# One table orders every operation of local attention and gated convolution, in smaller pieces

## The chip, the core and the metric

The kernel runs on one core of a Trainium2 chip. The metric is the device time of one execution in microseconds, less is better. TensorE (PE) multiplies, VectorE (DVE), ScalarE (ACT) and GpSimd (POOL) work on elements, SyncE (SP) issues the DMAs. Each engine takes its own queue in order and waits at an instruction until what it needs is there.

## The reference

For 4 batches, 8 heads, 768 positions and 64 dimensions: each query attends to the keys less than 16 positions away and to 24 block summaries (the maximum of the keys of 32 positions, the mean of the values). The result `x` goes through a causal depthwise convolution of 5 taps, whose sigmoid gates a projection of `x`; a second projection gives the output.

```python
k_sum = k.reshape(B, H, nb, block, D).max(axis=3)
v_sum = v.reshape(B, H, nb, block, D).mean(axis=3)
scores_l = where(abs(pos_q - pos_k) < 16, scale * q @ k.T, -1e9)
scores_s = scale * q @ k_sum.T + log(block)
a = softmax(concatenate([scores_l, scores_s], -1))
x = a @ concatenate([v, v_sum], 2)               # (B, S, 512)
gate = sigmoid(sum(conv_w[k] * xp[:, k:k + S] for k in range(5)))
out = (gate * (x @ w_val)) @ w_out
```

## The kernel before

The work is cut into 24 units: 4 batches, 3 thirds of the sequence (256 positions), 2 halves of the heads. Two units make a group `g`, 12 in all. Each stage of a unit has a function, called here by a short name that the new table uses too:

- S (`mm_s`, L311): scores on PE, 32 small matmuls, into the one PSUM buffer `s`. Half r holds one pair of heads.
- N (`snorm`, L328): mask and running minimum on DVE, 8 instructions, each with a read of its accumulator.
- E (`exps`, L342): 8 exps with row sums on ACT.
- R and M (`norm`): reciprocal of the sums on DVE (L350, L351), then two multiplications on POOL (L354) into `p`, which has three buffers.
- T and C (`tp` L367, `pcopy` L371): four transposes on PE per half into the one buffer `pt`, and its copy to `pts` on ACT. The second half waits for the first copy.
- X (`mm_x`, L387): probabilities by values on PE into the one buffer `x`.
- H, F and L (`xout`): on ACT the rounded part `xh` (L402) and the full `xf` (L403), on POOL the rest `xl` (L405). h is the halo of `xf` (L286, L288).
- I, A and G (`ginit` L419, `taps` L428, `gate` L436): the convolution. ACT starts the accumulator `g` (one PSUM buffer) with the last tap, DVE adds the other four for each of two head pairs in place, ACT takes the tanh.
- V, gf, gh and gl (`val_mm` L453, `val_ev` L460 and L467, `val_low` L476): value projection on PE (24 matmuls of two split parts; group 0 uses the weights unsplit), gating on DVE, split on ACT and POOL.
- O, oe and st (`out_mm` L491, `out_ev` L505 and L506): output projection on PE, scaling on ACT, store on SP.

`prep_k` makes the block maxima (ks, L129, on DVE) and copies them between the keys (kc, L139, POOL); `prep_v` sums the values on POOL (tr, L153) or DVE; `fill_vs` (f, L200) writes the means into the value tile `v` by DMA; `conv_w` and `split_w` turn the weights' 64-bit words into floats and split them (s, d, e, c, b on ACT, DVE, DVE, ACT, POOL).

The order of every queue is the order in which the program calls these functions: the scheduler is set to manual. The first 8 units are written out by hand, call by call. From unit 8 on `step(s)` is called: it puts X of unit s-2, one or two projections, S, N and E of unit s, T and C of unit s-1, then the taps and the tanh of unit s-2. The loads are a string `LOADS` and tables by step. All DMAs stand in SP's one queue.

Of the kernel before, what the change touches and what calls it, by code (L numbers as in the profile page):

```python
# [57 lines left out]


@with_exitstack  # L60
def tile_attention_then_gated_conv(
# [35 lines left out]
    ktile = {}  # L97
    vtile = {}
    vTt = {}

    def load_q0(pr):
# [11 lines left out]
    def load_vT(b, pr):
        t = ld.tile([P, S], F32, tag="vT", name=f"vT_{b}_{pr}")
        nc.sync.dma_start(t, vT[b, pr])
        vTt[b, pr] = t

    def load_v(g):
# [1 line left out]
        t = ld.tile([VROWS, TPU, DM], F32, tag="v", name=f"v_{g}")  # L120
        for e in range(VP):
            nc.sync.dma_start(t[:, 2 * e : 2 * e + 2], vw[b, th, e])
        vtile[g] = t

    def prep_k(b, pr):
        t = ktile[b, pr]
        ks = wk.tile([P, NB], F32, tag="ks", name=f"ks_{b}_{pr}")
# [47 lines left out]

    def place_vs0():
        for e in range(2):
            ps = ps_p.tile([P, DM], F32, tag="pp", name=f"vb_{e}")
# [4 lines left out]
            vblk[e] = t

    def prep_vs(b):
        ps = ps_p.tile([P, DM], F32, tag="pp", name=f"vsp_{b}")
# [4 lines left out]
        vsum[b] = t

    def fill_vs(g):
        b = g // NTH
        vr = vtile[g].rearrange("p (t e) c -> p e t c", e=2)
        for e in range(2):
            for half in range(2):
                off = OFF_A if (e == half) else OFF_B
                src = vsum[b][half * HB : half * HB + HB] if b else vblk[e][off : off + HB]
                nc.sync.dma_start(  # L200
                    vr[off : off + HB, e],
                    src.unsqueeze(1).broadcast_to([HB, TPU // 2, DM]),
                )
# [657 lines left out]
```

## Time and profile before

| | |
|---|---|
| median of 3 runs | 265.61 us (263.45 to 267.11) |
| span of the profiled execution | 262.0 us |
| around the span (median less span) | 3.6 us |
| busy: PE, ACT, DVE, POOL | 231.1, 193.0, 185.1, 151.8 us |
| instructions | 7326 |
| moved by DMA | 46.39 MB |

The span runs from the first to the last instruction of one profiled execution on the chip. Busy time is the time in which an engine had at least one instruction under way; the rest it waited or had nothing to do. The page lists the chain of work that ended last, and the trace gives each instruction's start, its length and what ended the idle time ahead of it.

### The profile page before, as it was taken

The numbers are of one execution on the slowest core, as the hardware profiler recorded it, in microseconds if no ns is written. First come the engines' busy times: TensorE is split into PE (matmuls) and PEld (weight loads), VectorE is DVE, ScalarE is ACT, GpSimd is POOL, SyncE is SP. The second block draws the span as 40 slices with busy tenths as digits, with TensorE's granted clock in tenths as the row PEclk, the third lists the DMA queues.
The fourth block names the chain that finished last, engine by engine and source line by source line (L and its number), as shares of the span: only waits on it lengthen the run. The fifth ranks groups of instructions, "written<-read, shape, count | busy, mean of one in ns | idle before, by whom it ended". The sixth has DMA issues, their size and how long they took to land.

```text
span 262.0 us, 7326 instructions
## 1 busy us (share of the span) xinstructions
PE 231.1 (88%) x2652; PEld 193.6 (74%) x2652; DVE 185.1 (71%) x692; ACT 193.0 (74%) x619; POOL 151.8 (58%) x212
## 2 busy tenths in 40 slices
PE   1258977889596999999999999999999999997994
PEld 1146866756482689888988898889889988986883
DVE  1866999597966687779776967797778667843610
ACT  1448994966648889888987898889878988875211
POOL 2243087767465788878663888887544744461410
PEclk9999999999777799999999999999999999999999
DMA  6999998175501967726118998171184511111012
GB/s 192 402 404 410 354 354 305 17 290 188 170 8 26 319 238 241 267 51 247 44 22 257 363 329 290 22 280 44 17 261 108 192 58 27 40 43 40 14 70 80
DMA packets 17028, 46.39 MB, mean 177 GB/s; under 512 B 2368, under 2 KB 3392, under 8 KB 16992
## 3 DMA queue, kind: packets, MB, share of 16 engines
q1 hardware_dynamic: 16992, 45.93, 50.9%
q8 instruction: 21, 0.34, 0.5%
q14 instruction: 15, 0.12, 0.2%
HBM read 37.46 MB, written 6.29 MB: 167 GB/s over the span
## 4 chain that ended last, share of the span: by engine, by line
PE 75%; ACT 10%; POOL 5%; issue 4%; DVE 2%; DMA 2%; SPq 0%; POOLq 0%; ACTq 0%; DVEq 0%
PE out L491 27%; PE val L453 22%; PE s L311 9%; PE x L387 8%; PE pt L367 8%; ACT p L342 4%; DMA k<-in_kT_dram 2%; POOL xl L405 2%; POOL p L354 1%; ACT pts L371 1%; DVE sn L328 1%; ACT wv L241 1%; ACT xf L403 1%; DVE ks L129 1%; POOL k L139 1%
## 5 line engine op out<-in xcount | busy, mean ns | idle before, releaser
L428 DVE SCALAR_TENSOR_TENSOR g<-xf,cwt,g 128x256 f32<-128x256 f32 x192 | 93.9, 489 | 13.9 <-ACT g L419 8.0
L342 ACT ACTIVATE p<-sn,nm 128x120 f32<-128x120 f32 x192 | 73.2, 386 | 10.9 <-DVE nm L328 10.9
L354 POOL TENSOR_TENSOR p<-p,ri 128x480 f32<-128x480 f32 x48 | 47.0, 1001 | 42.1 <-DVE ri L351 41.7
L328 DVE CUSTOM_DVE_ANT_0 sn<-s,mask 128x120 f32<-128x120 f32 x192 | 40.9, 278 | 33.3 <-PE s L311 33.3
L453 PE MATMUL val<-xh,wv 128*128 128x256 f32 x352 | 51.8, 289 | 0.7 <-ACT xh L402 0.7
L491 PE MATMUL out<-wo,gh 128*128 128x512 f32 x176 | 49.2, 418 | 2.0 <-ACT wo L241 1.2
L453 PEld LDWEIGHTS val<-xh,wv 128*128 128x128 f32 x352 | 45.6, 192 | 1.6 <-ACT xh L402 1.1
L405 POOL TENSOR_TENSOR xl<-xf,xh 128x512 fp32r<-128x512 f32 x22 | 28.3, 1288 | 23.3 <-ACT xf L403 23.3
L367 PE MATMUL pt<-ident,p 128*120 128x128 f32 x192 | 31.5, 289 | 11.0 <-ACT pts L371 7.6
L491 PEld LDWEIGHTS out<-wo,gh 128*128 128x128 f32 x176 | 32.1, 193 | 11.0 <-POOL wo L242 3.4
L311 PE MATMUL s<-k,qbd 64*64 64x120 f32 x768 | 27.7, 282 | 10.9 <-POOL k L139 10.9
L342 ACT ACTIVATION_READ_ACCUMULATOR p<-sn,nm 128x1 f32 x192 | 36.7, 191 | 0.0
L371 ACT COPY pts<-pt 120x512 f32<-120x512 f32 x48 | 27.6, 575 | 10.3 <-PE pt L367 10.3
L367 PEld LDWEIGHTS pt<-ident,p 128*120 128x120 f32 x192 | 21.7, 142 | 16.6 <-issue 7.3
L387 PEld LDWEIGHTS x<-pts,v 120*64 120x64 f32 x768 | 27.0, 141 | 9.2 <-issue 8.1
L476 POOL TENSOR_TENSOR gl<-gf,gh 128x512 fp32r<-128x512 f32 x22 | 28.5, 1298 | 6.6 <-ACT gh L467 6.6
L311 PEld LDWEIGHTS s<-k,qbd 64*64 64x64 f32 x768 | 20.9, 139 | 14.4 <-POOL k L139 12.6
L453 PE MATMUL val<-xl,wv 128*128 128x256 f32 x176 | 29.6, 288 | 1.8 <-POOL xl L405 1.7
L387 PE MATMUL x<-pts,v 120*64 120x64 f32 x768 | 30.7, 229 | 0.6 <-ACT g L419 0.5
L436 ACT ACTIVATE gt<-g 128x512 f32<-128x512 f32 x24 | 14.4, 599 | 22.0 <-DVE g L428 22.0
L153 POOL TENSOR_TENSOR vT<-vT 128x384 f32<-128x384 f32 (+3 forms) x44 | 25.6, 581 | 2.6
L453 PEld LDWEIGHTS val<-xl,wv 128*128 128x128 f32 x176 | 24.8, 191 | 2.6 <-POOL xl L405 2.1
(53 smaller groups left out, 268.2 us busy)
## 6 DMA issues: line engine op xcount, KB each, us to landing
v<-in_vw_dram SPq DMA_DIRECT2D x24, 512.0 KB
k<-in_kT_dram SPq DMA_DIRECT2D x16, 478.0 KB
vT<-in_vT_dram SPq DMA_DIRECT2D x16, 384.0 KB
out_dram<-ob SPq DMA_DIRECT2D x23, 256.0 KB
qbd<-in_qT_dram SPq DMA_DIRECT2D x11, 512.0 KB
raw_wv<-in_wv_dram SPq DMA_DIRECT2D x4, 512.0 KB
raw_wo<-in_wo_dram SPq DMA_DIRECT2D x4, 512.0 KB
v<-vs SPq DMA_DIRECT2D x36, 48.0 KB
```

What stands on the lines that cost most here:

```text
L311: nc.tensor.matmul(st[u]["sp"][64 * e : 64 * e + 64, h, c * KW : c * KW + KW], qbd[g % NQB][64 * h : 64 * h + 64, pr, i * QT : i * QT + QT ...
L328: nc.vector.tensor_tensor_reduce(s["sn"][:, n, :], s["sp"][:, h, c * KW : c * KW + KW], mask[:, mv, :], -1.0 / math.sqrt(D), 3.0e38, ALU.a ...
L342: nc.scalar.activation(s["p"][:, n, :], s["sn"][:, n, :], AF.Exp, bias=s["nm"][:, n : n + 1], scale=-1.0, accum_out=s["rs"][:, n : n + 1],)
L354: nc.gpsimd.tensor_tensor(s["p"][:, w], s["p"][:, w], ri[:, w].unsqueeze(2).broadcast_to([P, TPU, KW]), ALU.mult,)
L367: nc.tensor.transpose(s["pt"][:KW, i, :], s["p"][:, TPU * r + i, :], ident)
L371: nc.scalar.copy(s["pts"][:, TPU * r : TPU * r + TPU], s["pt"][:KW])
L387: nc.tensor.matmul(dst, v[:KW, i, c0 : c0 + D], src, start=True, stop=g > 0)
L405: nc.gpsimd.tensor_tensor(G["xl"][:, prs, :], x[:, prs, HALO:], G["xh"][:, prs, :].bitcast(F32), ALU.subtract)
L428: nc.vector.scalar_tensor_tensor(gt[:, r], x[:, pr, o : o + SG], cwt[:, pr, o : o + 1], gt[:, r], ALU.mult, ALU.add,)
L453: nc.tensor.matmul(pp[:, r], w, x, start=(n == 0), stop=(n == len(terms) - 1))
L476: nc.gpsimd.tensor_tensor(G["gl"][:, cos, :], gf, G["gh"][:, cos, :].bitcast(F32), ALU.subtract)
L491: nc.tensor.matmul(pp, x, w, start=(n == 0), stop=(n == len(terms) - 1))
```

## The change

All calls are replaced by one table of some 1,400 tokens, `ORDER`, and one small function per operation. A token such as `E.5.2` is unit 5, piece 2; the loop at the end calls the functions in the table's order, so every queue takes its subsequence. Tiles are made where they are first used. The pieces are smaller: N and E come in four pieces of two per unit, A in eight single taps, I in two halves, M in two, a load of `v` in two, a fill in four, and H, F, L, oe, st, gf, gh, gl, ks and kc stand each for itself. The arithmetic, the tile sizes and the buffer counts are the same.

```diff
-LOADS = "k0 q0 m k1 q1 n0 i k2 q2 n1 k3 q3 n2 n3 v0 c Q w0 w1 w2 w3 v1"
+ORDER = """
+k.0.0 q0.0 k.0.3 k.0.1 m q0.1 k.0.2 q0.3 ks.0.0 q0.2 w.3 kc.0.0 S.0.0 c ks.0.3 ks.0.1 q.1 i N.0.0
+n.0.3 kc.0.1 E.0.0 N.0.1 kc.0.3 S.0.1 E.0.1 ks.0.2 n.0.2 n.0.0 N.0.2 n.0.1 kc.0.2 E.0.2 N.0.3
...
-    def step(s, late=lambda: None):
-        u, t, x = s < NU, s - 1 < NU, s - 2 < NU
...
-            mm_s(s, 0)
-            mm_s(s, 1)
-            snorm(s, 0)
-            snorm(s, 1)
-        if t:
-            tp(s - 1, 0)
-        if u:
-            exps(s, 0)
...
+    def op_N(u, c):
+        b, th, hp = units[u]
+        sn = wt(("sn", u), [P, NP, KW], "sn")
+        nm = wt(("nm", u), [P, NP], "nm", bufs=4)
...
+        for h in range(2):
+            n = 2 * c + h
+            nc.vector.tensor_tensor_reduce(
...
+    def op_E(u, c):
+        p = wt(("p", u), [P, NP, KW], "p", bufs=3)
+        rs = wt(("rs", u), [P, NP], "rs", bufs=4)
+        for n in (2 * c, 2 * c + 1):
+            nc.scalar.activation(
...
+    def op_I(u, r):
+        gt = once(("g", u), lambda: ps_g.tile([P, 2, SG], F32, tag="g", name=f"g_{u}"))
...
+    def op_A(u, k):
+        r, o = divmod(k, NK - 1)
+        gt, pr = tiles["g", u][:, r], 2 * (u % NHP) + r
+        nc.vector.scalar_tensor_tensor(
+            gt, xf(u // NHP)[:, pr, o : o + SG], cwt[:, pr, o : o + 1], gt, ALU.mult, ALU.add
+        )
...
+    for token in ORDER.split():
+        name, *at = token.split(".")
+        ops[name](*(int(a) for a in at))
```

Three places of the queues. The names are tile, unit (or group and part) and a running number; `x8` is eight in a row.

ACT at the start, before (`p` is written by exps, `pts` by copies of transposes, `sc` by weight conversion):

```order
L342 ACTIVATE p_0_136,rs_0_138<-sn_0_135,nm_0_137 128x120 x8
L342 ACTIVATE p_1_185,rs_1_187<-sn_1_184,nm_1_186 128x120 x4
L371 COPY pts_0_217<-pt_0_0_218 120x512
L342 ACTIVATE p_1_185,rs_1_187<-sn_1_184,nm_1_186 128x120 x4
L371 COPY pts_0_217<-pt_0_1_240 120x512
L182 ACTIVATE vb0_259<-vb_0_254 120x512
L182 ACTIVATE vb1_266<-vb_1_261 120x512
L213 ACTIVATE sc_cw_285<-cwraw_116 128x20
L213 ACTIVATE sc_wv0_289<-raw_wv0_119 128x512
L371 COPY pts_1_293<-pt_1_0_294 120x512
L213 ACTIVATE sc_wv1_300<-raw_wv1_121 128x512
L403 COPY xf_0_338<-x_0_304 128x2x256
```

and now:

```order
L430 ACTIVATE p_0_133,rs_0_134<-sn_0_125,nm_0_126 128x120 x8
L347 ACTIVATE sc_wv3_184<-raw_wv3_104 128x512
L430 ACTIVATE p_1_204,rs_1_205<-sn_1_197,nm_1_198 128x120 x6
L347 ACTIVATE sc_cw0_236<-cwraw_117 128x20
L372 CAST wv_86<-wf_88 128x512
L430 ACTIVATE p_1_204,rs_1_205<-sn_1_197,nm_1_198 128x120 x2
L430 ACTIVATE p_2_262,rs_2_263<-sn_2_247,nm_2_248 128x120 x6
L454 COPY pts_0_302<-pt_0_0_255 120x512
L430 ACTIVATE p_2_262,rs_2_263<-sn_2_247,nm_2_248 128x120 x2
L347 ACTIVATE sc_wv2_324<-raw_wv2_178 128x512
L347 ACTIVATE sc_wv0_331<-raw_wv0_201 128x512
L454 COPY pts_0_302<-pt_0_1_315 120x512
```

The exps of units 2 and 3 stand ahead of the copies of unit 1 and of the first output of X; weights are taken in the order 3, 2, 0.

PE in the loop, before (one pass from X of unit 9; `s` scores, `pt` transposes, `val` and `out` projections):

```order
L387 MATMUL x_9_1583<-pts_9_1499,v_4_1065 64x64 x16
L311 MATMUL s_11_1621<-k_1_2_645,qbd1_82 64x120 x8
L311 MATMUL s_11_1621<-k_1_3_770,qbd1_82 64x120 x8
L367 MATMUL pt_10_0_1651<-ident_84,p_10_1472 120x128 x4
L453 MATMUL val_4_0_1678<-xh_4_1303,wv_88 128x256 x8
L453 MATMUL val_4_0_1678<-xl_4_1304,wv_88 128x256 x4
L453 MATMUL val_4_0_1678<-xh_4_1303,wv_88 128x256 x8
L453 MATMUL val_4_0_1678<-xl_4_1304,wv_88 128x256 x4
L367 MATMUL pt_10_1_1703<-ident_84,p_10_1472 120x128 x4
L491 MATMUL out_3_0_1723<-wo_89,gh_3_1409 128x512 x8
```

and now, the pass in which T of unit 8 stands:

```order
L450 MATMUL pt_8_0_1336<-ident_84,p_8_1055 120x128 x4
L399 MATMUL s_11_1343<-k_1_2_597,qbd1_82 64x120 x8
L399 MATMUL s_11_1343<-k_1_3_350,qbd1_82 64x120 x8
L467 MATMUL x_7_1366<-pts_7_1282,v_3_866 64x64 x16
L450 MATMUL pt_8_1_1392<-ident_84,p_8_1055 120x128 x4
L550 MATMUL out_1_0_1400<-wo_87,gh_1_1232 128x512 x8
L550 MATMUL out_1_0_1400<-wo_87,gl_1_1279 128x512 x4
L450 MATMUL pt_9_0_1452<-ident_84,p_9_1157 120x128 x4
L399 MATMUL s_12_1459<-k_2_0_1234,qbd0_81 64x120 x8
L399 MATMUL s_12_1459<-k_2_1_921,qbd0_81 64x120 x8
```

S of unit 11 stood beside T of unit 10 and stands beside T of unit 8; there is one projection between the two T pairs here where there were two.

DVE in the loop, before (`sn` masks, `g` taps, `ri` reciprocals, `gf` gating, `ks` maxima):

```order
L328 ISA sn_9_1319,nm_9_1321<-s_9_1318,mask_83 128x120
L328 ISA nm_9_1321 128x1
L328 ISA sn_9_1319,nm_9_1321<-s_9_1318,mask_83 128x120
L328 ISA nm_9_1321 128x1
L428 SCALAR_TENSOR_TENSOR g_7_1308<-xf_3_959,cwt_85,g_7_1308 128x256 x8
L350 TENSOR_SCALAR ri_9_1370<-rs_9_1322 128x8
L351 RECIPROCAL ri_9_1370<-ri_9_1370 128x8
L460 SCALAR_TENSOR_TENSOR gf_3_0_1407<-gt_3_958,val_3_0_1375 128x512
L129 TENSOR_REDUCE ks_2_0_1412<-k_2_0_1016 128x24
L328 ISA sn_10_1471,nm_10_1473<-s_10_1470,mask_83 128x120
L328 ISA nm_10_1473 128x1
L328 ISA sn_10_1471,nm_10_1473<-s_10_1470,mask_83 128x120
```

and now:

```order
L501 SCALAR_TENSOR_TENSOR g_6_1322<-xf_3_1226,cwt_85,g_6_1322 128x256 x6
L415 ISA sn_11_1414,nm_11_1415<-s_11_1343,mask_83 128x120
L415 ISA nm_11_1415 128x1
L415 ISA sn_11_1414,nm_11_1415<-s_11_1343,mask_83 128x120
L415 ISA nm_11_1415 128x1
L501 SCALAR_TENSOR_TENSOR g_6_1322<-xf_3_1226,cwt_85,g_6_1322 128x256
L415 ISA sn_11_1414,nm_11_1415<-s_11_1343,mask_83 128x120
L415 ISA nm_11_1415 128x1
L415 ISA sn_11_1414,nm_11_1415<-s_11_1343,mask_83 128x120
L415 ISA nm_11_1415 128x1
L501 SCALAR_TENSOR_TENSOR g_6_1322<-xf_3_1226,cwt_85,g_6_1322 128x256
L415 ISA sn_11_1414,nm_11_1415<-s_11_1343,mask_83 128x120
```

The eight taps of a unit are broken up by masks of a unit five later; before, eight masks stood in a row ahead of eight taps in a row.

## Rows read from the trace of the kernel before

**Rows 1.** The page: the span, and the busy time of the engines (share of the span, instructions).

```profile
span 262.0 us, 7326 instructions
...
PE 231.1 (88%) x2652; PEld 193.6 (74%) x2652; DVE 185.1 (71%) x692; ACT 193.0 (74%) x619; POOL 151.8 (58%) x212
```

**Rows 2.** Stretches of 20 us: length, busy us of PE, of PE's weight loads, of DVE, ACT and POOL (with the instructions), then the granted clock, the DMA share and GB/s.

```profile
0.00:20.00 20.00, 6.85 (x75) 4.87 (x75) 10.80 (x46) 7.78 (x31) 5.84 (x21) 1.00 0.92 334
20.00:40.00 20.00, 16.55 (x249) 13.94 (x247) 16.69 (x62) 18.12 (x59) 9.40 (x12) 1.00 1.01 374
...
60.00:80.00 20.00, 15.82 (x171) 11.79 (x164) 15.14 (x43) 11.69 (x34) 10.88 (x17) 0.83 0.30 104
...
100.00:120.00 20.00, 20.00 (x238) 17.88 (x237) 16.90 (x74) 17.53 (x61) 17.27 (x26) 1.00 0.59 196
```

**Rows 3.** The chain of waits, one pass of the loop: start, us, engine and line.

```profile
97.67 1.08 PE x L387 x32
98.75 0.98 PE s L311 x32
99.73 0.58 PE pt L367 x4
100.31 2.91 PE val L453 x24
103.22 0.44 PE pt L367 x4
103.66 2.80 PE out L491 x12
```

**Rows 4.** PE in order of time, the first 60 us: start, us, engine, line, operation, out<-in, shapes, count, and in brackets the idle time ahead and what ended it.

```profile
5.50 1.08 PE L311 MATMUL s<-k,qbd 64*64 64x120 f32 x16 [5.50 <-POOL k L139]
...
17.49 1.08 PE L311 MATMUL s<-k,qbd 64*64 64x120 f32 x16 [0.21 <-POOL k L139]
...
30.09 7.17 PE L453 MATMUL val<-xf,wf 128*128 128x256 f32 x32
...
59.56 0.64 PE L311 MATMUL s<-k,qbd 64*64 64x120 f32 x16
```

**Rows 5.** The same, 56 to 100 us and the end.

```profile
69.07 1.08 PE L367 MATMUL pt<-ident,p 128*120 128x128 f32 x4 [3.17 <-ACT pts L371]
...
81.54 0.60 PE L491 MATMUL out<-wo,gh 128*128 128x512 f32 x1 [1.22 <-ACT wo L241]
...
87.19 1.74 PE L491 MATMUL out<-wo,gl 128*128 128x512 f32 x4
...
240.65 0.74 PE L453 MATMUL val<-xh,wv 128*128 128x256 f32 x4 [0.69 <-ACT xh L402]
...
242.49 0.50 PE L453 MATMUL val<-xl,wv 128*128 128x256 f32 x2 [0.87 <-POOL xl L405]
...
257.34 1.10 PE L491 MATMUL out<-wo,gl 128*128 128x512 f32 x4
```

**Rows 6.** One stretch of 2 us, columns as in rows 2.

```profile
84.00:86.00 2.00, 1.96 (x5) 1.00 (x4) 1.67 (x4) 1.97 (x10) 2.00 (x3) 0.50 0.52 94
```

**Rows 7.** The start: the second K tile on the chain of waits (start, us), then the first mask on DVE and the first exp on ACT in order of time.

```profile
2.11 5.50 DMA k<-in_kT_dram
...
6.64 0.28 DVE L328 CUSTOM_DVE_ANT_0 sn<-s,mask 128x120 f32<-128x120 f32 x1 [1.70 <-PE s L311]
...
6.97 0.40 ACT L342 ACTIVATE p<-sn,nm 128x120 f32<-128x120 f32 x1 [4.95 <-DVE nm L328]
```

**Rows 8.** ACT in order of time: two exps in a row, four weight casts, copies of x, a wait for the transposes, and the tanh in the loop with the idle time ahead of it.

```profile
30.79 0.39 ACT L342 ACTIVATE p<-sn,nm 128x120 f32<-128x120 f32 x1
...
31.17 0.39 ACT L342 ACTIVATE p<-sn,nm 128x120 f32<-128x120 f32 x1
...
34.58 2.17 ACT L241 CAST wv<-wf 128x512 fp32r<-128x512 f32 x4
...
42.17 0.59 ACT L402 CAST xh<-x 128x512 fp32r<-128x512 f32 x1 [1.49 <-PE x L387]
42.65 0.59 ACT L403 COPY xf<-x 128x512 f32<-128x512 f32 x1
...
78.58 0.59 ACT L371 COPY pts<-pt 120x512 f32<-120x512 f32 x1 [2.64 <-PE pt L367]
...
96.88 0.60 ACT L436 ACTIVATE gt<-g 128x512 f32<-128x512 f32 x1 [0.92 <-DVE g L428]
```

**Rows 9.** DVE in order of time, one pass of the loop: the last mask of a unit, eight taps, and what stands behind them.

```profile
101.22 0.28 DVE L328 CUSTOM_DVE_ANT_0 sn<-s,mask 128x120 f32<-128x120 f32 x1
...
101.42 4.16 DVE L428 SCALAR_TENSOR_TENSOR g<-xf,cwt,g 128x256 f32<-128x256 f32 x8
105.49 0.16 DVE L350 TENSOR_SCALAR ri<-rs 128x8 f32<-128x8 f32 x1
...
106.38 0.95 DVE L129 TENSOR_REDUCE ks<-k 128x24 f32<-128x768 f32 x1
```

**Rows 10.** SP's waits (us in total, times, longest), and its issues in order of time.

```profile
SPq L200 <- DMA v<-in_vw_dram: 13.8, 5, 5.9
...
147.02 3.31 SPq L200 DMA_DIRECT2D v<-vs  x4
...
152.74 0.88 SPq L122 DMA_DIRECT2D v<-in_vw_dram  x2
```

More of the change, by code (lines that the diff above doesn't have):

```diff
@@ L95, in tile_attention_then_gated_conv, with once, wt @@
     cwt = cpool.tile([P, NPR, NK], F32, tag="cwt", name="cwt")
[L97 to L101, printed above, removed]
+    wide = wv.dtype != F32
+    units = [(b, th, hp) for b in range(B) for th in range(NTH) for hp in range(NHP)]
+    NG = B * NTH
+    tiles = {}
+    def once(key, make):
+        if key not in tiles:
+            tiles[key] = make()
+        return tiles[key]
+    def wt(key, shape, tag, dt=F32, bufs=None):
+        name = "_".join(str(k) for k in key)
+        kw = {} if bufs is None else dict(bufs=bufs)
+        return once(key, lambda: wk.tile(shape, dt, tag=tag, name=name, **kw))
@@ L113, in load_vT, with op_k @@
[L113 to L118, printed above, removed]
-        b, th = divmod(g, NTH)
[L120 to L127, printed above, removed]
+    def op_k(b, pr):
+        nc.sync.dma_start(ktile(b, pr)[:, :KTOT], kT[b, pr])
@@ L193, in fill_vs, with half0 @@
-    def fill_vs(g):
-        b = g // NTH
[L195 to L203, printed above, removed]
+    def half0(i, e):
+        offs = (OFF_A, OFF_B) if e == 0 else (OFF_B, OFF_A)
+        return [tiles["vpad"][:, i, e, off : off + HB] for off in offs]
@@ new lines, in op_VS, with op_vs, op_f @@
+    def op_VS(b):
+        ps = pp(("vsp", b), [P, DM])
+        for pr in range(NPR):
+            nc.tensor.transpose(ps[:NB, pr * P : pr * P + P], tiles["vsT", b, pr], ident)
+    def op_vs(b):
+        t = wt(("vs", b), [NB, DM], "vs", bufs=1)
+        nc.scalar.activation(t, tiles["vsp", b][:NB, :], AF.Copy, scale=1.0 / BLK)
+    def op_f(g, e, half):
+        b = g // NTH
+        vr = vtile(g).rearrange("p (t e) c -> p e t c", e=2)
+        off = OFF_A if (e == half) else OFF_B
+        src = (
+            tiles["vs", b][half * HB : half * HB + HB] if b else tiles["vblk", e][off : off + HB]
+        )
+        nc.sync.dma_start(
+            vr[off : off + HB, e], src.unsqueeze(1).broadcast_to([HB, TPU // 2, DM])
+        )
@@ L490, in out_mm, with op_oe @@
+            terms = [(gh[:, ci, rows], w[:, ci, :]) for ci in range(4) for w in (wh, wl)]
+            terms += [(gl[:, ci, rows], wh[:, ci, :]) for ci in range(4)]
         for n, (x, w) in enumerate(terms):
[L491 to L494 removed]
+            nc.tensor.matmul(ps, x, w, start=(n == 0), stop=(n == len(terms) - 1))
+    def op_oe(g, si):
+        ps = tiles["out", g, si]
+        ob = wt(("ob", g, si), [P, DM], "ob")
+        hd = DM // 2
+        if (g, si) == (NG - 1, 1):
+            nc.scalar.activation(ob[:, :hd], ps[:, :hd], AF.Copy, scale=0.5)
+            nc.vector.tensor_scalar(ob[:, hd:], ps[:, hd:], 0.5, None, ALU.mult)
+        else:
+            nc.scalar.activation(ob, ps, AF.Copy, scale=0.5)
```

825 lines of the change are left out of this document (289 added, 536 removed).

## The prediction

> **What bounds the kernel now.** I read the page's busy shares first [rows 1]: PE is busy 231.1 of 262.0 us, ACT 193.0, DVE 185.1. An average over stages says little, so next comes the table of stretches [rows 2]. From 100 us on PE is busy 20.00 of 20 us, until the tail: nothing that another engine does there matters as long as PE is not made to wait. Before that PE is idle for 13.2, 3.5 and 4.2 us in the first, second and fourth 20 us, and no engine is full. The chain of waits gives the price of a pass of the loop [rows 3]: X 1.08, S 0.98, first half of T 0.58, V 2.91, second half of T 0.44, O 2.80, together 8.79 us (the pass after it 8.74). So a unit costs PE 8.75 us, 24 units 210 us. Group 0 runs its projections on unsplit weights and X with a second matmul, which adds some 1.4 us for V (7.17 for two against 5.7, [rows 4]), as much for O and 1.0 for each of two X (twice the matmuls); I put the small transposes for `vb` and `vsp` at 2.8. **PE's work is about 217 us** at the full clock.
>
> PE's last matmul ends at 258.5 us [rows 5], so 41.6 us of PE's time hold no full-speed work. I split them by PE's queue. The first O on split weights (`out_mm(1,0)`) starts at 81.5 us [rows 5]. Ahead of it PE has done 8 S, 7 T, 6 X, 5 V, 2 O and the small transposes, 47.8 us at the full clock: **33.7 us behind**. That O then takes 7.4 us instead of 2.8: the granted clock reads 0.50 at 84 to 86 us [rows 6] and 0.83 on the mean of 60 to 80 [rows 2], 0.50 being the lower level (1.2 GHz); PE had stood still for 3.17 us before 69.07 and 1.22 before 81.54 [rows 5]. **4.6 us.** Near the end V(11,0) waits for `xh` and `xl` of the last unit, 0.69, 0.87 and an issue gap of 0.5, **2.1 us**. 33.7 + 4.6 + 2.1 is 40.4; the other 1.2 are scattered.
>
> **The change part by part.** Instructions of every kind stay as many as they were and keep their shapes; only the order of the five queues moves. So no work is priced anew; what is worked out is how far PE's queue lags its own work.
>
> *Loads.* The mask is now the fifth load of SP's queue, with three K tiles ahead of it instead of one. Before, the second K tile (1.27 MB into the queue) landed at 7.6 us [rows 7], and the loads then move 0.37 MB/us (374 GB/s, [rows 2]). The mask is now 1.78 MB in: 7.6 + 0.51/0.37 = 9.0 us. The first masks run at 9.3 instead of 6.64, the first exp at 9.55 instead of 6.97 [rows 7]: **ACT starts 2.6 us later**. What this buys is that all four K tiles are there: S of unit 1 is complete at 13 us, against 18.6 [rows 4].
>
> *Scores run ahead.* S of unit u now stands beside T of u-3 in the loop (before: u-1), so exps have work while T, copies and projections wait for each other. It costs no instruction; the three buffers of `p` carry it.
>
> *The ACT queue up to the first split O* (now `O.1.1`; before it stand ACT's ops to `gh.1.0`): 39 exp pieces at 0.76 (two exps, 0.38 from start to start), 15 copies at 0.48, 11 of x at 0.48, 12 inits at 0.45, 16 weight ops at 0.55, 5 tanh at 0.52, 8 others: **62.5 us** [rows 8]. *DVE's up to `gf.1.1`:* 40 mask pieces at 0.41, 40 taps at 0.51, 9 max reductions at 0.86, weights 9.1, the rest 10.5: **64 us** [rows 9]. PE's queue has only 55.7 us of work ahead of that O. So ACT and DVE, not PE, set the pace up to there, and both must be nearly full. I walked the three queues and POOL's by hand at these durations, each op starting when its engine is free and its producers are done. ACT begins at 9.55 and waits 3.6 us in ten places (the longest 0.6: for `C.3.0`, behind the first V, and for `oe.0.0`), so `gh.1.0` ends at 75.7; DVE ends `gf.1.1` at 71.2. `O.1.1` starts at 76.2 with 55.7 us done: **20.5 us behind**. One group later (`O.2.0`, DVE's `gf.2.1` at 88.0) the walk gives 90.9 less 70.3, 20.6. From there the queues of ACT and DVE need less per unit than PE (7.7 and 7.2 against 8.75), and the lag stays.
>
> *Taps.* Eight taps take 4.16 us, 0.49 each with 0.03 idle before the next, because each adds to the one before; the op behind the last starts 0.09 before it ends [rows 9]. Of the 168 places between two taps of a unit 62 now hold other work, 26 of them before `gf.2.1`: 26 x 0.12 = 3.1 us off DVE, which I leave out of the sum and set against waits that the walk missed.
>
> The Trainium skill ("VectorE: DVE Perf Modes", section on the DRAIN you can't avoid) says the next op doesn't start until the pipe is empty and that a semaphore between ops costs nothing extra; by it the inserted work would gain nothing. The rows just named show an overlap for an independent neighbour and none for a dependent one. By the page the sum stays as it is, by the rows it could be up to 3 us less.
>
> *Accumulator `g`.* It has one buffer: init of unit u+1 waits for tanh of u, tanh for the last tap. In most units one to five DVE ops stand between the last tap of u and the first of u+1 and cover most of tanh and init (0.52 + 0.45 and a copy or two); behind units 11 and 18 nothing does and DVE idles 1.6 us. DVE has 1.5 us per unit to spare there, so I take nothing.
>
> *Clock.* The walk has no PE wait over 1.5 us after 22 us; in the trace now 3.5 us of such waits between 20 and 40 us left the clock at 1.00 [rows 2]. I take the **4.6 us** as gone. At the start the same 16 matmuls of S take 1.08 us at 5.50 and at 17.49, and 0.64 at 59.56 [rows 4]: early work runs slow now too, though the record reads 1.00. The first X may fall into that: up to 2 us, I take 1.
>
> *Tail.* Between X of the last unit and `V.11.0` now stand `V.10.1`, `O.9.1`, `O.10.0`, 8.4 us; the copies and the low part behind X need some 8.0 because `F.23` stands behind `gh.10.1`. The **2.1 us** go.
>
> *Fills on SP.* Fills of the summary rows into `v` (0.83 us of SP each, [rows 10]) now stand behind loads of later groups, which wait for X: `f.5.1.1` behind `v.6`, `f.7` behind `v.8`, `f.9` behind `v.10`. Two loads, a store and the fill are 2.1 us of issue after X.9, their 1.3 MB 3.5 us at 0.37 MB/us, so it lands 5.6 to 6 us after X.9; X.10 comes 6.8 us after. Nothing, if that holds; 1 to 3 us in each of four places if it doesn't.
>
> **Sum.** 217 + 20.5 = 237.5 for the last matmul; 3.5 behind it as now (262.0 - 258.5): 241. Plus 1 for the slow start and 3 for waits that a walk by hand overlooks (now's loop has an ACT wait of 0.92 us per unit for the last tap that no sum shows [rows 8]): **a span of 245**. The runs' median lies 3.6 us over the span of the profiled execution (265.61 against 262.0): **249 us**, 6% less. Bounds: the sums without any wait (ACT to `C.1.1`, 27.0 with its start at 8.5, against 10.5 us of PE work; DVE to `gf.2.1`) leave PE 16.5 us behind, 237 and 241 us with what lies around; if PE stays 33.7 behind and only clock and tail go, 217 + 33.7 + 3.5 + 3.6 = 258.
>
> **The rivals.** *Two full engines wait for each other.* Up to 90 us ACT and DVE are both at 90% or more in my walk; in the trace now they reach 18.1 and 16.7 of 20 at best there [rows 2]. If pieces make each wait for the other as the whole blocks did, the lag is 33.7 again: 258, and with one long PE wait and the slow clock behind it 262, no difference that can be measured (2% here is 5.3 us). For: no stretch of rows 2 has two engines over 90% before PE is full. Against: the ACT idle before 80 us is in a few long waits for whole blocks (up to 2.64 us, [rows 8]), which the pieces break.
>
> *SP's order.* The fills come late at each group: 4 places x 3 us = 12, 261 us. For: fills waited 13.8 us for the loads ahead of them already [rows 10]. Against: they stand a unit ahead of their X.
>
> *Slower.* The one buffer of `g` becomes the loop's bound: with mask pieces, gf and reductions between a unit's own taps, first tap to last takes 4.6 to 4.8 us by the walk instead of 4.16, then come tanh, init and what ACT does between them, each behind whatever stands ahead in ACT's queue. If this ring takes 10.0 us instead of 8.75, 22 units cost 27 us: 276. It decides from 9.75 us, where forecast plus 22 x 1.0 us is 271. For: ACT waits for the last tap already [rows 8]. Against: by the walk the ring takes 5.9, 7.3 and 6.2 us in units 4 to 6.
>
> **How the numbers follow.** Forecast with its small variants (241 to 255) 0.68; mutual waits 0.14 (255 to 262); SP 0.08; ring 0.10 (half of it over 271). Faster by over 2% (under 260.3): 0.68 + 0.10 + 0.03 = 0.81; within 2%: 0.04 + 0.05 + 0.04 = 0.13; slower: 0.06. The range runs from the sums without waits, 241, to 261, which takes in the first two rivals' middles.
>
> **What would show it.** In the trace after: first exp near 9.5 us; ACT and DVE over 17.5 of 20 us from 20 to 80; the first split O near 76 to 79 us and its 12 matmuls in 2.8 us; granted clock 1.00 throughout; PE full from there on, without a wait at V(11,0). Wrong if PE shows waits of over 0.5 us per unit after 100 us: then the ring (DVE waiting for init) or the fills (PE waiting for SP's DMAs) ended them.

## The result, and the profile after

The changed kernel takes **251.82 us** (median of 4 runs, 251.55 to 252.76) beside 265.66 us for the kernel before (4 runs on the same chip); the ratio is 0.949 with a 95% interval of 0.943 to 0.955. The forecast was 249.0 us with a range of 241 to 261. Executions of one kernel fall into a faster and a slower state; times and ratios here are of the faster one, and so are the traces but for those of o_tp and g2_loop. The page of the changed kernel, to set beside [rows 1]:

```profile
span 250.1 us, 7309 instructions
...
PE 224.8 (90%) x2652; PEld 192.3 (77%) x2652; DVE 183.5 (73%) x692; ACT 189.8 (76%) x619; POOL 152.2 (61%) x212
```

Each engine is busy for as long as before to within 7 us; the span is 11.9 us shorter, the median 13.8. Stretches of 20 us, columns as in [rows 2]:

```profile
20.00:40.00 20.00, 18.26 (x308) 15.76 (x308) 19.83 (x89) 19.55 (x72) 18.27 (x33) 1.00 0.97 351
40.00:60.00 20.00, 18.72 (x249) 15.74 (x246) 19.86 (x65) 17.99 (x62) 16.68 (x25) 1.00 0.98 363
60.00:80.00 20.00, 18.74 (x208) 14.06 (x209) 18.35 (x75) 18.18 (x59) 15.08 (x19) 1.00 0.67 213
80.00:100.00 20.00, 18.86 (x240) 15.74 (x238) 17.85 (x67) 17.94 (x61) 16.43 (x27) 1.00 0.46 154
...
120.00:140.00 20.00, 20.00 (x273) 18.29 (x262) 15.80 (x70) 17.19 (x57) 16.16 (x26) 1.00 0.55 172
...
160.00:180.00 20.00, 18.32 (x266) 15.55 (x265) 15.73 (x71) 16.44 (x57) 8.70 (x9) 1.00 0.36 109
```

From 20 to 60 us DVE is busy 19.83 and 19.86 of 20 and ACT 19.55 and 17.99; before, no engine was full there. The granted clock reads 1.00 in each stretch, where 60 to 80 us had 0.83 (the trace holds no clock record before 24.4 us, and a stretch shows 1.00 where it has none). PE, on the other hand, is full at 120 to 140 us (20.00; before, from 100 on) and has a hole again at 160 to 180. PE in order of time, columns as in [rows 4]:

```profile
21.12 1.88 PE L399 MATMUL s<-k,qbd 64*64 64x120 f32 x32 [1.15 <-DVE nm L415]
...
79.04 0.65 PE L450 MATMUL pt<-ident,p 128*120 128x128 f32 x4 [1.06 <-ACT pts L454]
79.56 2.14 PE L550 MATMUL out<-wo,gh 128*128 128x512 f32 x8
81.54 1.09 PE L550 MATMUL out<-wo,gl 128*128 128x512 f32 x4
...
119.69 1.05 PE L399 MATMUL s<-k,qbd 64*64 64x120 f32 x32 [0.73 <-DVE nm L415]
...
176.02 1.05 PE L399 MATMUL s<-k,qbd 64*64 64x120 f32 x32 [0.94 <-DVE g L501]
...
229.46 1.10 PE L521 MATMUL val<-xh,wv 128*128 128x256 f32 x8
...
245.42 1.10 PE L550 MATMUL out<-wo,gl 128*128 128x512 f32 x4
```

The first O on split weights (`O.1.1`) starts at 79.56 with 55.7 us of full-clock work ahead of it: PE is 23.9 us behind, where the forecast had 20.5 and the kernel before 33.7 [rows 5]. It ends at 82.6, at the full clock. V of the last group (229.46) stands in a row with its neighbours. The last matmul ends at 246.5, 29.5 us behind 217. So 5.6 us are lost behind `O.1.1`: 4.3 in eight waits of over 0.2 us (the two largest are the 0.94 and 0.73 shown), the other 1.3 are scattered. A span of 250.1 and 1.7 around it are the 251.8.

### The profile page after: what moved, and what is told of

Read it like the earlier page. It is cut to its first block, busy times and chain, and to the rows that moved or that the text cites. A ratio compares the mean times of both kernels' runs of the same rounds, so it can differ in the third digit from the quotient of the medians.

```text
span 250.1 us, 7309 instructions
## 1 busy us (share of the span) xinstructions
PE 224.8 (90%) x2652; PEld 192.3 (77%) x2652; DVE 183.5 (73%) x692; ACT 189.8 (76%) x619; POOL 152.2 (61%) x212
## 4 chain that ended last, share of the span: by engine, by line
PE 44%; DVE 33%; ACT 13%; issue 3%; DMA 3%; POOL 1%; SPq 1%; ACTq 0%; DVEq 0%; POOLq 0%
PE out L550 16%; PE val L521 15%; DVE g L501 14%; DVE sn L415 7%; PE x L467 5%; ACT p L430 4%; PE s L399 4%; PE pt L450 4%; DMA k<-in_kT_dram 3%; ACT g L496 3%; DVE ks L246 2%; DVE ri L437 2%; DVE wf L364 2%; ACT pts L454 2%; DVE vpad L281 1%
## 5 line engine op out<-in xcount | busy, mean ns | idle before, releaser
L501 DVE SCALAR_TENSOR_TENSOR g<-xf,cwt,g 128x256 f32<-128x256 f32 x192 | 93.0, 484 | 24.3 <-ACT g L496 17.5
L430 ACT ACTIVATE p<-sn,nm 128x120 f32<-128x120 f32 x192 | 74.0, 394 | 11.9 <-DVE nm L415 11.9
L443 POOL TENSOR_TENSOR p<-p,ri 128x480 f32<-128x480 f32 x48 | 47.6, 1003 | 33.9 <-DVE ri L438 24.8
L521 PE MATMUL val<-xh,wv 128*128 128x256 f32 x352 | 49.9, 283 | 0.0
L415 DVE CUSTOM_DVE_ANT_0 sn<-s,mask 128x120 f32<-128x120 f32 x192 | 43.6, 275 | 3.6 <-PE s L399 3.3
L550 PE MATMUL out<-wo,gh 128*128 128x512 f32 x176 | 45.7, 402 | 0.0
L399 PE MATMUL s<-k,qbd 64*64 64x120 f32 x768 | 29.3, 293 | 16.8 <-DVE nm L415 7.7
L535 POOL TENSOR_TENSOR gl<-gf,gh 128x512 fp32r<-128x512 f32 x22 | 28.4, 1293 | 23.9 <-ACT gh L530 23.7
L399 PEld LDWEIGHTS s<-k,qbd 64*64 64x64 f32 x768 | 22.7, 147 | 21.5 <-POOL k L259 13.1
L430 ACT ACTIVATION_READ_ACCUMULATOR p<-sn,nm 128x1 f32 x192 | 38.0, 198 | 0.0
L270 POOL TENSOR_TENSOR vT<-vT 128x384 f32<-128x384 f32 (+3 forms) x44 | 27.0, 613 | 5.7 <-DMA vT<-in_vT_dram 3.1
L526 DVE SCALAR_TENSOR_TENSOR gf<-gt,val 128x512 f32<-128x512 f32 x24 | 16.4, 682 | 17.5 <-PE val L521 12.5
L521 PE MATMUL val<-xl,wv 128*128 128x256 f32 x176 | 27.9, 279 | 0.0
L550 PE MATMUL out<-wo,gl 128*128 128x512 f32 x88 | 24.2, 396 | 0.0
```

What stands on the lines that cost most here:

```text
L399: nc.tensor.matmul(sp[64 * e : 64 * e + 64, h, c * KW : c * KW + KW], qbd[g % NQB][64 * h : 64 * h + 64, pr, i * QT : i * QT + QT], ktile( ...
L415: nc.vector.tensor_tensor_reduce(sn[:, n, :], tiles["s", u][:, h, c * KW : c * KW + KW], mask[:, mv, :], -1.0 / math.sqrt(D), 3.0e38, ALU.add,
L430: nc.scalar.activation(p[:, n, :], tiles["sn", u][:, n, :], AF.Exp, bias=tiles["nm", u][:, n : n + 1], scale=-1.0, accum_out=rs[:, n : n + 1],
L443: nc.gpsimd.tensor_tensor(p[:, w], p[:, w], ri[:, w].unsqueeze(2).broadcast_to([P, TPU, KW]), ALU.mult)
L501: nc.vector.scalar_tensor_tensor(gt, xf(u // NHP)[:, pr, o : o + SG], cwt[:, pr, o : o + 1], gt, ALU.mult, ALU.add)
L521: nc.tensor.matmul(ps[:, r], w, x, start=(n == 0), stop=(n == len(terms) - 1))
```

## The experiments

Each run changes the table (1,172 tokens) alone. "Lag" is a start or an end on PE less PE's work up to there, worked out as in the prediction (55.7 us ahead of `O.1.1` where the table's PE queue is that of the changed kernel, 47.8 in the kernel before, 53.3 to 57.2 in s_f, s_tp and s_r). The lags are read from the profiled execution, which lies up to 2.3 us off the median beside it. In h2_newloop the join lies ahead of its first split O.

| kernel | us | ratio to before, 95% | lag at first split O | lag at the end |
|---|---|---|---|---|
| before | 265.7 | | 33.7 | 41.5 |
| changed | 251.8 | 0.943 to 0.955 | 23.9 | 29.5 |
| h1_newhead | 260.8 | 0.979 to 0.992 | 25.9 | 39.7 |
| h2_newloop | 272.6 | 1.024 to 1.039 | 46.1 | 49.6 |
| t1_taps | 276.9 | 1.041 to 1.054 | 30.7 | 54.5 |
| p1_halves | 262.3 | 0.983 to 0.997 | 25.7 | 40.1 |
| s_f | 257.3 | 0.964 to 0.970 | 30.7 | 35.0 |
| s_tp | 261.5 | 0.976 to 0.990 | 31.9 | 41.0 |
| s_r | 256.2 | 0.959 to 0.966 | 31.5 | 35.1 |
| g2_loop | 254.9 | 0.954 to 0.967 | 24.6 | 34.8 |

**The start of one table with the loop of the other.** The order of the kernel before can be written as the same kind of table: in the two runs the part that is taken from it has the same rows in the same order on each queue. So either part can be joined to the other.

```diff
 h1_newhead:  ... T.7.1 A.5.6 E.9.3 gl.1.0 O.1.1
-A.5.7 F.6 R.9 C.7.1 N.10.1 M.8.0 ks.2.2 G.5 I.6.0 ...      (changed table)
+st.0.1 gf.2.0 gh.2.0 A.5.7 G.5 O.1.0 oe.1.0 st.1.0 F.6 ... (order before)
 h2_newloop:  ... A.5.7 R.7 M.7.0 M.7.1 G.5
-q.5 k.2.1 n.2.1 O.1.0 X.6 oe.1.0 st.1.0 H.6 ...            (order before)
+n.2.2 q.5 tr.2.2 k.2.2 k.2.1 tr.2.0 n.2.3 S.8.0 S.8.1 ...  (changed table)
```

> The changed table up to its first O on split weights (O.1.1), then everything that is left in the order of the kernel before (its loop with scores one unit ahead, whole halves of masks and exps, eight taps in a row). Theory (the gain is made in the first 80 us and by the clock, and any loop that keeps PE fed keeps it): O.1.1 starts near 79.6 us as in the changed kernel, 23.9 us behind its work, at the full clock; the old loop adds its 1.2 us of scattered waits and 2.1 us in the tail: the last matmul at 217 + 23.9 + 3.3 = 244 us, about 249.5 us in all, no slower than the changed kernel's 251.8. Rival (the pieces and the scores three units ahead are what keeps PE fed in the loop): PE waits 0.3 us or more per unit after 80 us, 255 us or more.

> The kernel before up to its tanh of unit 5 (its whole hand-written start, so also the weights' work), then everything that is left in the order of the changed table. Theory: PE is 33.7 us behind at the first O on split weights, which runs at half rate again (4.6 us), and the changed loop loses nothing more, since ACT and DVE have then 14 us more to get ahead: last matmul at 217 + 38.3 = 255.3, about 259 to 261 us in all, 2% faster than the kernel before at most. Rival (the loop of the changed table loses 5.6 us wherever it starts): 264 to 266 us. Second rival (the loop was the gain): 255 us or less.

Measured 260.8 and 272.6 us. The first lies in the range of its rival (255 us or more), but not by its reason, a wait of PE in every unit; the second is slower than anything that was expected. The stretches behind the join and later, of h1_newhead and then of h2_newloop, columns as in [rows 2]:

```profile
80.00:100.00 20.00, 13.33 (x89) 10.90 (x87) 10.22 (x25) 9.83 (x25) 8.72 (x9) 0.83 0.32 112
...
120.00:140.00 20.00, 20.00 (x261) 17.16 (x259) 15.52 (x60) 16.90 (x54) 11.11 (x16) 1.00 0.30 83
```

```profile
80.00:100.00 20.00, 9.62 (x145) 8.23 (x146) 11.45 (x66) 13.83 (x56) 14.92 (x21) 0.57 0.68 228
...
120.00:140.00 20.00, 19.12 (x252) 16.73 (x248) 16.55 (x61) 17.03 (x57) 14.55 (x20) 1.00 0.65 223
```

From 80 to 100 us PE stands idle for 6.7 and 10.4 us, and the clock reads 0.83 and 0.57. What it waits for there, DVE and ACT of h1_newhead and PE of h2_newloop in order of time:

```profile
89.50 4.17 DVE L500 SCALAR_TENSOR_TENSOR g<-xf,cwt,g 128x256 f32<-128x256 f32 x8 [6.31 <-ACT g L495]
```

```profile
93.69 0.60 ACT L506 ACTIVATE gt<-g 128x512 f32<-128x512 f32 x1 [3.72 <-DVE g L500]
```

```profile
89.81 1.88 PE L398 MATMUL s<-k,qbd 64*64 64x120 f32 x32 [7.37 <-DVE nm L414]
```

In h1_newhead the taps wait 6.31 us for the init of their unit and the tanh then 3.72 us for the taps; in h2_newloop S waits 7.37 us for masks. From 120 us on the loop of before keeps PE full again up to 220 us, and the changed loop loses 0.9 us at 120 to 140 and 2.5 us up to 220. So the loops, once they run, add little to the lag, as the prediction had it; the join does. Joined like this, with nothing moved to fit, the new start keeps 1.5 of the 5.1% with the old loop (interval 0.8 to 2.1%), and the changed loop behind the old start is 3% slower than the kernel before.

**The pieces taken back one by one.**

```diff
 t1_taps, DVE around unit 5:
-gf.1.1 N.10.2 R.8 A.5.0 N.10.0 A.5.1 A.5.2 A.5.3 A.5.4 A.5.5 N.10.3 A.5.6 A.5.7
+gf.1.1 N.10.2 R.8 N.10.0 N.10.3 A.5.0 A.5.1 A.5.2 A.5.3 A.5.4 A.5.5 A.5.6 A.5.7
 p1_halves, ACT there:
-I.5.0 gh.1.1 E.9.0 I.5.1 H.6 E.9.2 C.7.0 gh.1.0 E.9.3
+I.5.0 gh.1.1 E.9.0 E.9.1 I.5.1 H.6 C.7.0 gh.1.0 E.9.2 E.9.3
```

> The changed table with the eight taps of every unit in a row again, at the place of the last one; what stood between them now stands ahead of them, in its order. Theory (an independent neighbour starts 0.09 us before its predecessor ends, a dependent tap doesn't): 26 places before the second split group cost DVE 2.3 us there, and DVE is full from 15 to 71 us, so 1.0 to 2.3 us slower than the changed kernel: 253 to 254 us. Rival (mixing gains nothing and only makes a unit's taps longer, so the one buffer of g comes free later): the same or faster, 249 to 252 us.

> The changed table with masks and exps as whole halves again: the two mask pieces of a half at the place of the first, its two exp pieces at the place of the last; nothing else moves. Theory (the pieces break the waits of ACT and DVE for each other): the lag at O.1.1 grows from 23.9 us by 2 to 5 us, 254 to 257 us. Rival (scores three units ahead do it, and a piece's place matters little): within 1 us of the changed kernel, 251 to 253 us.

Measured 276.9 and 262.3 us, far more than either theory had. The waits (engine and line, what for, us in total, times, longest) of the changed kernel, of t1_taps and of p1_halves:

```profile
DVE g L501 <- ACT g L496: 17.5, 20, 3.5
...
ACT gt L507 <- DVE g L501: 12.3, 8, 4.4
...
ACT g L496 <- DVE g L501: 3.3, 5, 1.1
DVE sn L415 <- PE s L399: 3.3, 5, 1.2
...
PE pt L450 <- ACT pts L454: 2.4, 4, 1.1
```

```profile
ACT gt L506 <- DVE g L500: 47.6, 23, 6.5
...
DVE sn L414 <- PE s L398: 21.0, 10, 6.0
```

```profile
PE pt L449 <- ACT pts L453: 10.1, 10, 2.0
...
ACT g L495 <- DVE g L500: 8.5, 10, 1.6
```

With the taps behind the masks that stood among them, DVE waits 21.0 us for scores (3.3 in the changed kernel) with the taps queued behind; the tanh, next in the one buffer of `g`, then waits 47.6 us instead of 12.3, and PE ends 54.5 us behind. Of that only 6.8 us (30.7 against 23.9) arise ahead of `O.1.1`, the rest in the loop. With whole halves it is the copies of `pt` and the inits that come late: PE waits for copies ten times, not four, and ACT's inits for taps ten times, not five. This is the rival of engines that wait for each other; in this table it is held off by the place of single pieces. Both moves leave the instructions as they were, so what they cost is order.

**Other orders.** Is it then the size of the pieces, or the order found for them? Four tables were made by walking the queues at the durations of the rows and moving one operation at a time where the walk got shorter.

> The pieces of the changed table (quarters of masks and exps, single taps) in another order on all five queues, found by walking the queues at the durations of the traces, each operation starting when its engine is free and its producers are done; the first 34 loads keep their order. Theory (what is left of PE's lag, 23.9 us at O.1.1 and 5.6 us lost after it, is order and no work of any engine): the walk gives a span of 240, about 241.7 us. It starts its first exp later than the changed kernel (12 us instead of 10.4), so if ACT's late start sets the time, as the prediction put it, this must not be faster: 252 us. Rival (the pace is the work of ACT and DVE before O.1.1): 250 to 252 us.

> Whole halves of masks and exps and all eight taps of a unit in a row, as in the kernel before, scores as far ahead as the order wants, and the order of all five queues found anew by the same walk for these blocks. Theory A (the place of an operation in its queue counts, the size of the pieces doesn't; the whole halves alone, 262.3 us, and the taps in a row alone, 276.9 us, were slow because they were put into an order made for pieces): the walk gives 242.3, about 244 us, faster than the changed kernel. Theory B (whole blocks make ACT and DVE wait for each other in any order): 255 us or more.

> As the run before it (whole halves, taps in a row), and the scores of unit u stand behind X of unit u-2 as in the loop of the kernel before (from unit 7 on), with the 34 first loads of SP in its order too, the mask third. Only places of whole blocks differ from the kernel before. Theory A (order alone): the walk gives 244.5, about 246 us. Theory C (scores three units ahead are what fills ACT and DVE): 256 to 262 us.

> The changed table word for word up to O.1.1, what is left behind it in another order found by the walk. Theory (the 5.6 us that PE loses behind O.1.1, in 80 to 120 and 160 to 180 us, are waits of the order: DVE for the init of g, PE for masks of the unit before): PE stays 23.9 us behind: 217 + 23.9 + 3.6 behind the last matmul + 1.7 around the span = 246 us (the walk: 246.6). Rival (they are contention or work that no order removes): 251 to 252 us.

```diff
 g1_loop, SP's queue:
-v.5.1 v.5.0 n.3.2 f.5.0.1 f.5.0.0 f.5.1.0 k.3.1 v.6.1
+v.5.1 f.5.0.1 f.5.1.0 k.3.0 st.0.1 f.5.0.0 n.3.1 f.5.1.1 v.5.0
```

Measured 289.7, 285.7, 290.0 and 282.8 us; they settle nothing on pieces, because the walk had also moved SP's queue. In them 23 to 28 of the 44 fills stand ahead of a load of the `v` tile that they write to, so the load overwrites those summary rows and X computes without them; and transfers came late. A wait of X on PE and SP's issues in o_f:

```profile
111.32 0.48 PE L466 MATMUL x<-pts,v 120*64 120x64 f32 x4 [7.21 <-DMA v<-vs]
```

```profile
43.40 2.59 SPq L326 DMA_DIRECT2D v<-vb  x3
52.80 0.81 SPq L226 DMA_DIRECT2D v<-in_vw_dram  x2
```

X waits 7.2 us for one fill. The last two lines show how long a fill can take: three are issued by 46.0 us, and the load behind them, which writes the same tile, starts at 52.8. They took 6.8 us to land behind the loads issued ahead of them, where the prediction's step on fills had 3.5 for 1.3 MB. This is the price of the rival "SP's order", which the changed table does not pay: in it no X waits for a transfer.

With SP's queue put back (as in the changed table in s_f and s_tp, as in the kernel before in s_r), three of them again:

```diff
 DVE around the taps of unit 1:
 changed: A.1.0 R.4 A.1.1 A.1.2 N.6.3 A.1.3 A.1.4 N.6.1 A.1.5 ks.1.3 A.1.6 N.6.2 A.1.7
 s_f:     ks.1.3 N.6.0 N.6.3 R.4 N.6.2 N.6.1 A.1.4 A.1.5 A.1.6 A.1.0 ks.1.2 A.1.1 A.1.2
 s_tp:    N.6.2 N.6.3 ks.1.2 R.5 N.6.0 N.6.1 A.1.0 A.1.1 A.1.2 A.1.3 A.1.4 A.1.5 A.1.6
 s_r:     N.4.1 N.4.2 N.4.3 A.1.0 A.1.1 A.1.2 A.1.3 A.1.4 A.1.5 A.1.6 A.1.7 ks.1.0 R.4
```

> The pieces of the changed table, SP's queue word for word as in the changed table (the four orders before this one moved SP's loads and fills and PE waited up to 11 us for them), the queues of PE, ACT, DVE and POOL in another order found by the walk. Theory (what is left of PE's lag is order): the walk gives a span of 244 to 245.5, about 246 to 247 us. Rival (the work of ACT and DVE ahead of O.1.1 is the bound that is left): 250 to 252 us.

> Whole halves of masks and exps and the eight taps of every unit in a row, with SP's queue as in the changed table and the other four queues in an order found for these blocks. Theory A (the place of an operation in its queue counts, not the size of the piece): 244 to 245.5 by the walk, about 246 to 247 us, as the pieces in their own new order (run s_f) and no slower than the changed kernel. Theory B (whole blocks make ACT and DVE wait for each other in any order): 255 us or more.

> Whole halves, eight taps in a row, SP's queue as in the kernel before, and from unit 7 on the scores of unit u behind X of unit u-2 as in its loop: of the three parts of the change none is there, only places of whole operations on PE, ACT, DVE and POOL differ from the kernel before. Theory A (order alone): 246.7 to 248.1 by the walk, about 248 to 250 us, as fast as the changed kernel. Theory C (scores three units ahead are what fills ACT and DVE): 256 to 262 us.

Measured 257.3, 261.5 and 256.2 us. By the numbers s_tp lies where theory B had it (255 us or more) and s_r at the fast end of theory C. But the walk was 6 to 15 us short in all three, for the pieces of s_f too, so being slower than the walk does not tell whole blocks from pieces. Two things are left. First, s_r has whole halves of masks and exps, eight taps in a row and, from unit 7 on, scores one unit ahead, and is still 3.7% faster than the kernel before (0.959 to 0.966): 9.5 of the 13.8 us can be had without these three parts of the change. It is not the whole blocks of the kernel before alone: the halves of I stand apart in 13 of 24 units, those of M in 12, H and F in 14 of 22, and ahead of unit 7 the scores of units 2, 3 and 5 stand one X earlier. Second, its loop keeps PE fed without quarters or single taps; what it lacks lies ahead of 80 us. Stretches and PE of s_r:

```profile
20.00:40.00 20.00, 15.83 (x247) 13.02 (x239) 15.22 (x56) 16.35 (x56) 6.88 (x6) 0.74 0.95 354
...
80.00:100.00 20.00, 20.00 (x230) 16.90 (x230) 17.60 (x63) 17.20 (x59) 12.22 (x14) 1.00 0.46 145
```

```profile
30.00:32.00 2.00, 2.00 (x21) 1.36 (x22) 1.36 (x2) 1.01 (x2) 0.92 (x1) 0.50 0.80 262
```

```profile
25.80 0.64 PE L398 MATMUL s<-k,qbd 64*64 64x120 f32 x16
29.85 1.11 PE L449 MATMUL pt<-ident,p 128*120 128x128 f32 x4 [3.40 <-POOL p L442]
30.89 1.08 PE L398 MATMUL s<-k,qbd 64*64 64x120 f32 x16
```

PE stands still for 3.40 us before 29.85, the same 16 matmuls of S take 1.08 instead of 0.64 us behind it, and the granted clock is 0.50 at 30 to 32 us and 0.74 over 20 to 40. The changed kernel's longest PE wait behind 22 us is the 1.06 ahead of 79.04, and its clock stays at 1.00. How much each part of the change is worth with an order made for it is not settled: s_f (quarters, single taps, scores ahead) and s_r (none of them in its loop) differ by 1 us.

**The loop's own loss.** The last run keeps the changed table up to `O.1.1` and on SP.

```diff
 g2_loop, PE from O.1.1 on:
-O.1.1 T.8.0 S.11.0 S.11.1 X.7 T.8.1 O.1.0 T.9.0 S.12.0 S.12.1 X.8 T.9.1 V.3.0 O.2.0
+O.1.1 T.8.0 S.11.1 X.7 T.8.1 S.11.0 O.1.0 T.9.0 S.12.1 X.8 S.12.0 T.9.1 V.3.0 O.2.0
```

> The changed table word for word up to O.1.1 and on SP's whole queue; behind O.1.1 the same pieces on PE, ACT, DVE and POOL in another order, found by the walk. Theory (the 5.6 us that PE loses behind O.1.1 in the changed kernel, in 80 to 120 and 160 to 180 us, are waits of its order, around the one buffer of g and for masks of the unit before): O.1.1 starts near 79.6 as there, PE is full from there, last matmul at 217 + 23.9 = 241, span 244.5 to 246.7, about 246.5 us. Rival (the loss is contention for memory or transfers that no order of these four queues removes): 250 to 252 us as the changed kernel.

Measured 254.9 us, 3.0 us slower than the changed kernel. In the trace `O.1.1` starts at 80.3 and PE is then all but full to 130 us (19.5 and 20.0 of 20 us from 80 to 120), as the walk has it, until this, ACT, PE and SP in order of time, and then SP and ACT of the changed kernel:

```profile
131.72 0.60 ACT L559 ACTIVATE ob<-out 128x512 f32<-128x512 f32 x1 [3.35 <-DMA out_dram<-ob]
```

```profile
132.37 1.85 PE L520 MATMUL val<-xh,wv 128*128 128x256 f32 x8 [1.95 <-ACT ob L559]
```

```profile
123.18 0.42 SPq L568 DMA_DIRECT2D out_dram<-ob  x1
131.05 0.82 SPq L326 DMA_DIRECT2D v<-vs  x1
131.97 0.45 SPq L568 DMA_DIRECT2D out_dram<-ob  x1
```

```profile
123.49 0.42 SPq L569 DMA_DIRECT2D out_dram<-ob  x1
```

```profile
133.25 0.59 ACT L560 ACTIVATE ob<-out 128x512 f32<-128x512 f32 x1
```

ACT needs the buffer of an earlier output row and waits 3.35 us until its store has landed; V needs the PSUM buffer that this output leaves, so PE waits 1.95 us, and its 8 matmuls take 1.85 us, 1.10 elsewhere. ACT goes on at 131.72, before the store of 131.97 is issued, so it waited for the one of 123.18: issued behind four loads, it landed some 8 us later. The fill of 131.05 waited for one of these loads to land, which kept SP from issuing anything for 7.5 us. The changed kernel issues the same store at 123.49 and comes to its next output only at 133.25, without a wait. SP's queue is the same in both; the new order of ACT and PE asks for the buffer before the transfers give it back. Neither theory had it: not the ring of `g`, and not transfers that cost as much in any order.

The trace is of an execution of 257.2 us with a mean granted clock of 0.993; those behind the 254.9 have 0.999 to 1.00. How much of the 3.0 us this wait makes is therefore not shown, and neither is it shown that the 5.6 us of the changed loop are free to take.

## Why the prediction was right, and where its terms were off

- *PE's work sets the end, and the lag is made in the first 80 us.* Held: 9.8 us of the 12.0 us that the lag fell by lie ahead of `O.1.1`. Of the signs it named, ACT and DVE over 17.5 of 20 us from 20 to 80 and the clock came out; PE was not full behind that O (18.86 of 20 us at 80 to 100).
- *Loads, 2.6 us.* Off: first mask at 10.07, first exp at 10.38, not 9.3 and 9.55. The step took the landing of the mask alone; on DVE the third reduction (9.20, 0.95 long) stands ahead of the first mask piece. S of unit 1 is complete at 15.2 us, not 13.
- *Walk of ACT's queue, 62.5 us and 3.6 us of waits.* ACT ends `gh.1.0` at 79.5, not 75.7: 0.8 from the first exp, 2.2 from waits (eleven, 5.8 us in all) and some 0.8 from work. The walk's longest wait was 0.6 us; four of the measured ones are longer: 0.87 at 15.56 for a mask, 0.70 at 45.13 for the last tap, and two of those that follow, ACT and DVE in order of time:

```profile
10.38 0.39 ACT L430 ACTIVATE p<-sn,nm 128x120 f32<-128x120 f32 x1 [8.37 <-DVE nm L415]
...
58.38 0.69 ACT L347 ACTIVATE sc_wo<-raw_wo 128x512 f32<-128x512 f32 x1 [0.94 <-DVE wf L364]
...
70.80 0.48 ACT L496 ACTIVATE g<-xf,cwt 128x256 f32<-128x256 f32 x1 [0.16 <-DVE g L501]
...
76.76 0.48 ACT L496 ACTIVATE g<-xf,cwt 128x256 f32<-128x256 f32 x1 [0.87 <-DVE g L501]
...
78.89 0.62 ACT L530 CAST gh<-gf 128x512 fp32r<-128x512 f32 x1
```

```profile
9.20 0.95 DVE L246 TENSOR_REDUCE ks<-k 128x24 f32<-128x768 f32 x1 [0.39 <-DMA k<-in_kT_dram]
10.07 0.27 DVE L415 CUSTOM_DVE_ANT_0 sn<-s,mask 128x120 f32<-128x120 f32 x1
...
75.49 0.44 DVE L501 SCALAR_TENSOR_TENSOR g<-xf,cwt,g 128x256 f32<-128x256 f32 x1
75.84 0.27 DVE L415 CUSTOM_DVE_ANT_0 sn<-s,mask 128x120 f32<-128x120 f32 x1
...
76.04 0.28 DVE L415 CUSTOM_DVE_ANT_0 sn<-s,mask 128x120 f32<-128x120 f32 x1
...
76.25 0.48 DVE L501 SCALAR_TENSOR_TENSOR g<-xf,cwt,g 128x256 f32<-128x256 f32 x1
77.28 2.06 DVE L501 SCALAR_TENSOR_TENSOR g<-xf,cwt,g 128x256 f32<-128x256 f32 x4 [0.55 <-ACT g L496]
```

The one at 58.38 waits for the join of a weight, for the buffer behind it. Those at 70.80 and 76.76 are a round trip: in 15 units the init of the second half stands behind one to four of the unit's taps, so it waits for the tap (both write one PSUM tile), and the next tap waits for the init, which costs DVE 0.55 us at 77.28. These three waits add up to 1.97 us, near the 2.2, but the walk's own ten are not known one by one. Its waits were the term that was mis-sized most: `O.1.1` starts 3.4 us later than forecast.
- *"From there the lag stays", with 3 us allowed.* Short: 5.6 us are lost. ACT and DVE have little to spare at 80 to 100 us (17.9 of 20 busy), so some of their waits reach PE; the loss is small beside the 9.8 us, and the rest of the step held.
- *Clock, 4.6 us.* Held: 1.00 in every stretch to 240 us, `O.1.1` in 3.1 us instead of 7.4. That early work runs slow "though the record reads 1.00" was misread: there is no clock record that early, 20.3 us being the first in the kernel before. *Tail, 2.1 us.* Held: V of the last group (229.46) has no wait.
- *Taps.* The four taps at 77.28 take 2.06 us, 0.52 from one to the next; the mask at 75.84 starts 0.35 after the tap at 75.49 and 0.09 before its end, the tap at 76.25 0.07 before the end of the mask ahead of it. So an independent neighbour does overlap, as the prediction read from [rows 9]. The prediction cited the Trainium skill ("VectorE: DVE Perf Modes", section on the DRAIN you can't avoid) without the end of that paragraph: a next op that is not held back starts earlier. With that the rows agree. t1_taps shows that the overlap is not what the mixing is worth in this table.
- *Ring of `g`.* DVE's waits for the init rose from 8.0 us in 4 places to 17.5 in 20, yet the only wait of PE that the trace puts down to taps is the 0.94 us at 176.02. The rival was no bound, but the term was not the nothing that the sum had.
- *Around the span.* 1.7 us instead of 3.6. In every execution on record, of every kernel here, the time is 1.73 to 1.85 us over that execution's own span (263.74 with 262.0 in the kernel before); the 3.6 set the median beside the span of an execution below it. For the same reason the traces show 11.9 of the 13.8 us. With it the sum of the prediction, 248.6 before rounding, becomes what was measured: +3.4 at `O.1.1`, +1.6 behind it (5.6 instead of the 4 allowed for the slow start and for waits), +0.1 behind the last matmul and -1.9 around the span are +3.2, 251.8. So part of two misses was hidden by a third: that the forecast lies within 3 us is in part luck. Two small sums are off without weight: the second K tile ends 1.29 MB into the queue, not 1.27, and the terms of PE's work add up to 217.6, put at 217 throughout.

## What to carry to other kernels

Where PE's work is fixed, price a new order by how far PE is behind at the first place where it could run full, and check behind that place who has no slack. A table of places is one thing: taking one of its ideas back, or joining it to another loop, measures the fit and not the idea. Walk the transfers with the rest, up to their landing: a store issued behind four loads landed 8 us later and held PE by way of ACT.

## What the runs showed of the hardware

- Three fills of 48 KB took 6.8 us from the last issue to landing while loads ran (o_f), and a store of 256 KB behind four loads some 8 us (g2_loop), so a small transfer is not a fast one.
- 32 matmuls of S took 1.88 us at 21.12 and 1.05 at 119.69; the clock reads 1.00 in both stretches, but the trace has no record before 24.4 us.
- One wait of 3.40 us at 26 to 30 us was followed in s_r by a granted clock of 0.50 at 30 to 32 us and 0.74 on the mean of 20 to 40; the waits of the changed kernel behind 22 us, 1.06 at most, by none below 1.00.
